# An mLSTM cell feeding a GELU layer: another order of the front's steps, and the second sum of w_out in the middle of the second up projection

## The chip, the cores and the metric

The kernel runs on one core of one Trainium2 chip. The metric is device time in microseconds (us) of one execution. The kernel before has a median of 518.63 us over 11 runs (517.47 to 519.23).

A core has five engines that matter here: TensorE (PE in the profile; its weight loads are shown apart as PEld), VectorE (DVE), ScalarE (ACT), GpSimd (POOL) and SyncE (SP), which here only issues DMAs. Each works through its own queue of instructions in order, and waits on semaphores for the others.

## The reference

Two blocks follow each other. The first is a recurrent cell with batch 4, 8 heads, 768 steps and head size 40:

```python
for t in range(S):
    m_new = np.maximum(f_gate[:, :, t] + m, i_gate[:, :, t])
    f_stab, i_stab = np.exp(f_gate[:, :, t] + m - m_new), np.exp(i_gate[:, :, t] - m_new)
    C = f_stab[:, :, None, None] * C + i_stab[:, :, None, None] * np.einsum('bhd,bhe->bhde', vt, kt)
    n = f_stab[:, :, None] * n + i_stab[:, :, None] * kt
    ...
    y[:, :, t] = sigmoid(o_gate[:, :, t]) * h_tilde / np.maximum(np.abs(nq), 1.0)
```

Its result, as x with 3072 rows of 320, goes through `gelu(x @ w_in) @ w_out` with w_in 320 x 2048 and w_out 2048 x 320. The weights arrive as float64, and the kernel converts them from their bits.

## The kernel before, in words

The 768 steps are cut into six chunks of 128. For each chunk and each of the four batch entries the cell is worked out in matrix form; then the 512 tokens of the chunk (4 x 128) go through the up projection, the GELU and the down projection. The cell of chunk c+1 is worked out beside the down projection of chunk c.

Chunks 1 to 5 use a Strassen-like scheme: `summed_up` makes seven products in place of eight for the up projection, `down_steps` seven for the down projection. These need sums of blocks of w_in (`in_sum`), of x (`sum_x`), of the hidden values (`hidden_sums`) and of w_out (`weight_sum`). Chunk 0 is done with plain products, because the sums aren't there yet.

The first part of the program, called the front below, does all this together: the gates, the conversion of 26 pieces of the weights, the cells of chunks 0 and 1, and both projections of chunk 0. Its order is written out by hand in the string `FRONT`; `play` takes its words one after the other, and each issues instructions on several engines. Every engine's queue therefore has the order of the string. The words are:

- `P n` fetches piece n of the weights; `L n` loads q and k, `O n` loads v and the output gate; `B n` loads a broadcast of the running maxima. All go through SP's queue in this order.
- `E` and `N` work out the gates of the chunks behind the first (each with a store through SP's queue), `D` and `Q` turn the decays (`decays_turned`: transposes on PE, copies on DVE, a product, a copy).
- `K` is the first half of the conversion of the next piece (`conv_one`: three instructions on DVE, two on ACT), `J` the second half (`conv_two`: two on DVE, then the fetch of the piece four further on). Pieces 1 to 10 are w_in (512 columns wide), 11 to 26 are the rows of w_out (320 wide). Below, J4 is the fourth `J`.
- Small letters are the cell of chunk 0 with the batch entry behind them, capitals that of chunk 1: `m` mask (POOL), `w` decay weights (eight exponentials on ACT; in chunk 0 also products on PE), `g` sigmoid of the output gate, `t` transposes of k and q (PE) and their copies (ACT), `s` scores (PE) and their product with the weights (DVE, line 399), `c` state (PE; line 430 on ACT in chunk 0), `v` values (PE), `y` the end of the cell (DVE), `x` the transpose into xT (PE, ACT).
- `A` and `U` are the up projection of chunk 0 for the first and the second half of the tokens, in four steps each (`up_step`, lines 530 to 549). Two steps behind each other are issued together, a single one when the next other word comes. `F` is one of the 16 steps of chunk 0's down projection, `Z` one of the eight sums of w_in.
- `I n` (`keep_clock`) sets how many products of the identity with itself the next word with a PSUM bank makes into that bank ahead of its own work (`unread`, line 315). Nobody reads them. A later `I` ahead of that word overwrites the number. In the string before, 25 products are made that way, two instructions each in the profile.

[...] `ps_mm` has two buffers for each of the tags a and b. The scores of an even batch entry take both buffers of tag a until line 399 has read them, and `U` steps 1 and 3 take the same two; `A` and `U` alternate between a and b. `ps_h` has two buffers for `c` and `v`.

`FRONT` is played once. Then, for each further chunk, come `summed_up` and the string `DOWN`. For chunk 1 the kernel makes `weight_sum(1)` ahead of `summed_up` and `weight_sum(2)` behind it (eight subtractions of 128x160 on DVE each, line 508), and hands out sums 3 and 4 over `DOWN`. `summed_up` works in two groups of two column blocks, (0, 2) and (4, 6); within the second group it makes `hidden_sums` of the first, and at its end those of the second. The second product of the down projection (p6) reads sum 2.

Of the kernel before, what the change touches and what calls it, by code (L numbers as in the profile page):

```python
# [22 lines left out]


FRONT = """
    O0 g0 L0 I6 P0 E I6 I1 P1 I1 w0 t0 I1 I2 I2 L1 I2 N I1 I3 K I1 w1 I5 I2 D Q I6 I3 L2 s0 O2 P2 I3 O1 P3 I5 I1 t1
    I2 I2 w2 c0 I1 J v0 K K s1 I1 L3 I2 I5 w3 I2 t2 I6 I2 I8 I3 I2 I3 I3 y0 O3 v1 J I1 g1 x0 c1 K y1 s2 I7 O4 I1 L4
    I1 B5 t3 g3 I3 J I2 x1 g2 B4 s3 v2 I4 I1 I6 I2 I5 I6 I2 c2 c3 y2 v3 x2 M0 K J y3 G0 L5 O5 A L6 K J J x3 M1 T0 W0
    O6 A K S0 K C0 J H W1 L7 T1 M2 O7 U U M3 K J Z V0 K T2 G1 A J J S1 K C1 Z W2 W3 A J K Z S2 C2 V1 K T3 J K Y0 J U
    U K J Z S3 J G2 Y1 K C3 K Z J F F F K F J J F K Z F J F F G3 K J K X0 K J J B8 K K J J V2 Y2 V3 K J F K X1 F F F  # L30
    F F Y3 Z J Z B9 F X2 X3 F"""
DOWN = """
    M0 Z M1 T0 W0 F F T1 W1 Z G3 Z F S0 Z S1 C0 M2 Z C1 G1 G0 M3 V0 Y0 Z V1 W2 Z F F T2 W3 F T3 F G2 Z Y1 S2 S3 C2
    V2 C3 Y2 V3 F F Y3 X0 F F X1 X2 F F X3 F"""
# [3 lines left out]
def kernel(  # L38
# [18 lines left out]
    B, H, S, D = q.shape  # L57
# [442 lines left out]
    def weight_sum(n):  # L500
        x, y = {1: (Bm[0][1], Bm[0][0]), 2: (Bm[1][1], T[1]), 3: (Bm[1][1], Bm[0][1])}.get(n) or (Bm[1][0], T[2])
        if n == 4:

            parts = [raw.tile([P, 3, HD], F32, name="t4", tag=tag) for tag in ("sig", "pow", "sig")]
            T[4] = lambda j: parts[j // 3][:, j % 3, :]

        def step(j):
            nc.vector.tensor_tensor(out=T[n](j), in0=x(j), in1=y(j), op=OP.subtract)  # L508

        return [lambda j=j: (step(j), step(j + 1)) for j in range(0, HF, 2)]  # L510
# [10 lines left out]
    def hidden_sums(g, f0, f1):  # L521

        (a11, a21), (_, a22) = [[g.t[:, HF * e + f0:HF * e + f1, HT * h:HT * (h + 1)] for h in range(2)]
                                for e in range(2)]
        s1, s2 = [t[f0 // (HF // 2)][:, f0 % (HF // 2):f0 % (HF // 2) + f1 - f0, :] for t in (g.s1, g.s2)]
        nc.vector.tensor_tensor(out=s1, in0=a21, in1=a22, op=OP.add)
        nc.vector.tensor_tensor(out=s2, in0=s1, in1=a11, op=OP.subtract)
        nc.vector.tensor_tensor(out=a21, in0=a11, in1=a21, op=OP.subtract)
# [24 lines left out]
    def first_up_steps(h):  # L553

        def step(k):
            ups.append((len(ups) + len(tags_next) % 2, (2 * k, 2 * k + 2, HT * h, HT * h + HT)))
            if len(ups) == 2:
                first_up()

        return [lambda k=k: step(k) for k in range(HF // 2)]  # L560
# [12 lines left out]
    def in_sum(i):  # L573
        f, (a11, a12), (a21, a22) = slice(WP * (i // 4), WP * (i // 4 + 1)), *[[w_in[:, x, e, :] for x in range(NX)]
                                                                               for e in range(2)]
        s1, s2, s4 = in_sums
        to, x, y, op = ((s1, a21, a22, OP.add), (s2, s1, a11, OP.subtract), (a21, a11, a21, OP.subtract),
                        (s4, a12, s2, OP.subtract))[i % 4]
        nc.vector.tensor_tensor(out=to[:, f], in0=x[:, f], in1=y[:, f], op=op)

    def x_blocks():
        return [[xT[:, x, HT * h:HT * (h + 1)] for h in range(2)] for x in range(NX)]
# [4 lines left out]
        for to, x, y in ((t1, b12, b11), (t2, b22, t1), (b12, b22, b12), (t4, b21, t2)):  # L587
            nc.vector.tensor_tensor(out=to, in0=x, in1=y, op=OP.subtract)

    def summed_up(g):  # L590
        (a11, s3), (a12, a22) = [[w_in[:, x, e, :] for e in range(2)] for x in range(NX)]
        s1, s2, s4 = in_sums
        (b11, t3), (b21, b22) = x_blocks()
        t1, t2, t4 = x_sums
        def product(to, lhs, rhs, f0, first, last):

            for j in range(2):
                nc.tensor.matmul(to[:, j, :], lhs[:, (f0 + j) * P:(f0 + j + 1) * P], rhs, start=(first and j == 0),  # L598
                                 stop=(last and j == 1), skip_group_check=True)

        def products(f0, to_sum):

            blk = [[g.t[:, HF * e + f0:HF * e + f0 + 2, HT * h:HT * (h + 1)] for h in range(2)] for e in range(2)]
            c11, c12, c21, c22 = [pool.tile([P, 2, HT], F32, name="pu", tag=tag)
                                  for pool, tag in ((ps_tr, "tr"), (ps_h, "h"), (ps_mm, "a"), (ps_mm, "b"))]
            product(c11, a11, b11, f0, True, False)
            nc.scalar.copy(out=blk[1][1], in_=c11)  # L607
            product(c12, s2, t2, f0, True, True)
            nc.vector.tensor_tensor(out=blk[0][0], in0=c12, in1=blk[1][1], op=OP.add)  # L609
            product(c21, s1, t1, f0, True, True)  # L610
            nc.vector.tensor_tensor(out=blk[0][1], in0=c21, in1=blk[0][0], op=OP.add)
            product(c22, s3, t3, f0, True, False)
            nc.vector.tensor_tensor(out=blk[1][0], in0=c22, in1=blk[0][0], op=OP.add)
            if to_sum > 0:
                hidden_sums(g, f0 - 4, f0 - 2)
            product(c11, a12, b21, f0, False, False)
            product(c12, s4, b22, f0, True, False)
            product(c21, a22, t4, f0, True, False)
            return f0, blk, ((c11, c21), (c12, c22))

        def rest(f0, pair, h):
            for j in range(2):
                for e in range(2):
                    nc.tensor.matmul(pair[e][:, j, :], w_rest[halves[e], (f0 + j) * P:(f0 + j + 1) * P],  # L624
                                     xT[halves[e], NX, HT * h:HT * (h + 1)], start=False, stop=(j == 1),
                                     skip_group_check=True)

        for group in ((0, 2), (4, 6)):

            sets = [products(f, group[0]) for f in group]  # L630
            for h in range(2):
                for f, _, pairs in sets:
                    rest(f, pairs[h], h)
            for _, blk, ((c11, _), _) in sets:
                nc.scalar.activation(out=blk[0][0], in_=c11, func=AF.Gelu)  # L635
            add_to = lambda blk, e, h, x, y: (
                nc.vector.tensor_tensor(out=blk[e][h], in0=x, in1=y, op=OP.add),  # L637
                nc.scalar.activation(out=blk[e][h], in_=blk[e][h], func=AF.Gelu))  # L638
            for _, blk, ((_, c21), _) in sets:
                add_to(blk, 1, 0, c21, blk[1][0])  # L640
            for _, blk, (_, (c12, c22)) in sets:
                add_to(blk, 1, 1, c22, blk[0][1])
                add_to(blk, 0, 1, c12, blk[0][1])
        hidden_sums(g, HF - 4, HF)
# [4 lines left out]
    def first_down_steps(g):  # L649
        po = []  # L650

        def row(f):

            if f == 0:
                po.extend(ps_mm.tile([P, DM], F32, name="po", tag="ab"[b // 2]) for b in range(B))
            for b in range(B):
                nc.tensor.matmul(po[b], g.t[:, f, b * L:(b + 1) * L], w_out[:, f, :], start=(f == 0),  # L657
                                 stop=(f == NF - 1))
                if f == NF - 1:
                    if b % 2 == 0:  # L660
                        o_sb = outp.tile([P, 2, DM], F32, name="o_sb", tag="o_sb")
                    nc.scalar.copy(out=o_sb[:, b % 2, :], in_=po[b])
                    send(0, b, o_sb[:, b % 2, :])

        return [lambda f=f: row(f) for f in range(NF)]
# [71 lines left out]
    def in_turn(steps):  # L737
        todo = list(steps)
        return lambda: todo.pop(0)() if todo else None

    def cell_steps(c, letters):
# [8 lines left out]
                 A=in_turn(first_up_steps(0)), U=in_turn(first_up_steps(1)), F=in_turn(first_down_steps(first_g)),  # L750
                 K=in_turn(lambda i=i: conv_one(i) for i in n_pieces), H=sums_begin,
                 J=in_turn(lambda i=i: conv_two(i) for i in n_pieces), Z=in_turn(lambda i=i: in_sum(i) for i in range(8)))
    steps |= cell_steps(0, "mwgtscvyx") | cell_steps(1, "MWGTSCVYX")
    play(FRONT, steps)
    for c in range(1, NCH):
        g, later = Hidden(True), []
        if c == 1:
            for step in weight_sum(1):
                step()
        summed_up(g)  # L760
        if c == 1:
            for step in weight_sum(2):
                step()
            later = weight_sum(3) + weight_sum(4)
        steps = dict(F=in_turn(down_steps(c, g)), Z=in_turn(later))
        if c + 1 < NCH:
            steps |= cell_steps(c + 1, "MWGTSCVYX")
        play(DOWN if c + 1 < NCH else "F " * 14, steps)
# [30 lines left out]
```

## Time and profile before

| what | value |
|---|---|
| median of 11 runs | 518.63 us |
| the profiled execution | 517.57 us, of which the profile's span is 515.8 us |
| PE busy | 501.2 us (97%) |
| DVE busy | 342.5 us (66%) |
| ACT busy | 253.0 us (49%) |
| front (to the first product of `summed_up`) | 0 to 133.19 us |
| chunks 1 to 5 | 133.19 us to the end |
| granted TensorE clock, mean | 0.993 |

All times below are from the start of the span. A row of the list of instructions in order of time has the start, the duration, the engine, the line, the operation, the output and the inputs, the shapes, the number of instructions, and in brackets how long the engine sat idle before and what released it. Matmuls overlap, so that a row's duration is longer than the distance to the next row; sums are made with the distances. The chain of work that ended last gives start, duration, engine and line.

### The profile page before, as it was taken

How to read it: one execution, taken by the hardware profiler on the slowest of the kernel's cores; microseconds unless marked ns; L12 is line 12 of the kernel's file. 1: busy time of each engine (PE TensorE's matmuls, PEld its weight loads, DVE VectorE, ACT ScalarE, POOL GpSimd, SP SyncE). 2: the span in 40 equal slices, each digit the busy share in tenths (PEclk: the TensorE clock that was granted, in tenths of full speed). 3: DMA queues.
4: the chain of work that ended last, by engine and by line, in shares of the span. 5: the costliest groups of instructions: out<-in, count | busy, mean ns of one | idle time of the engine just before them, and what ended most of it. 6: DMA issues, size and time to landing. Idle time of an engine off the chain costs nothing.

```text
span 515.8 us, 10990 instructions
## 1 busy us (share of the span) xinstructions
PE 501.2 (97%) x4486; PEld 452.0 (88%) x4486; DVE 342.5 (66%) x696; ACT 253.0 (49%) x522; POOL 61.2 (12%) x98
## 2 busy tenths in 40 slices
PE   4899999999999999999999999999999999999997
PEld 3787888777888999988999988999988999988997
DVE  7689888999667987347668347678337657237621
ACT  7695999543344960152980132982123882124300
POOL 3001000001200235000045000053000021000000
PEclk9799999999999999999999999999999999999999
DMA  8999971259800244900124910124920020000001
GB/s 174 182 172 200 209 170 50 81 155 223 139 0 1 84 112 60 169 0 2 63 97 67 167 31 1 42 83 81 164 54 2 3 80 2 27 27 0 1 2 51
DMA packets 111442, 41.62 MB, mean 81 GB/s; under 512 B 101184, under 2 KB 104416, under 8 KB 111392
## 3 DMA queue, kind: packets, MB, share of 16 engines
q1 hardware_dynamic: 111392, 40.92, 37.8%
q8 instruction: 35, 0.57, 0.5%
q14 instruction: 15, 0.12, 0.1%
HBM read 36.90 MB, written 4.01 MB: 79 GB/s over the span
## 4 chain that ended last, share of the span: by engine, by line
PE 90%; DVE 6%; ACT 2%; issue 1%; DMA 0%; SPq 0%; DVEq 0%
PE po L680 29%; PE pu L598 24%; PE pu L624 7%; PE po L657 7%; PE pu L539 5%; PE ps L396 4%; PE ph L445 4%; PE pt L374 3%; PE pf L420 2%; PE pf L415 2%; PE pu L545 1%; PE px L471 1%; DVE M L195 1%; DVE g L637 1%; DMA i_sb<-in_i_gate_dram 0%
## 5 line engine op out<-in xcount | busy, mean ns | idle before, releaser
L680 PE MATMUL po<-w_out,g 128*128 128x160 f32 x640 | 91.5, 299 | 0.0
L680 PEld LDWEIGHTS po<-w_out,g 128*128 128x128 f32 x640 | 88.0, 190 | 0.3 <-DVE g L637 0.3
L598 PE MATMUL pu<-xT,w_in 128*128 128x256 f32 x240 | 58.9, 381 | 0.0
L637 DVE TENSOR_TENSOR g<-pu,g 128x512 f32<-128x512 f32 x60 | 40.5, 690 | 24.3 <-PE pu L624 22.8
L598 PEld LDWEIGHTS pu<-xT,w_in 128*128 128x128 f32 x240 | 45.0, 190 | 7.5 <-ACT g L638 1.7
L360 ACT ACTIVATE W<-Mb,aT 128x128 f32<-128x128 f32 x160 | 48.9, 391 | 0.1
L472 ACT COPY xT<-px 128x384 f32<-128x384 f32 x24 | 10.9, 476 | 76.9 <-PE px L471 76.9
L680 PE MATMUL po<-w_sums,sums 128*128 128x160 f32 x320 | 47.4, 302 | 0.3 <-DVE w_sums L508 0.3
L399 DVE TENSOR_TENSOR W<-ps,W 128x512 f32<-128x512 f32 x48 | 30.3, 685 | 22.1 <-PE ps L396 20.4
L680 PEld LDWEIGHTS po<-w_sums,sums 128*128 128x128 f32 x320 | 44.0, 190 | 0.9 <-DVE w_sums L508 0.5
L335 POOL TENSOR_SCALAR_AFFINE_SELECT Mb<-Mb 128x1024 f32<-128x1024 f32 x20 | 22.6, 1138 | 174.3 <-DMA Mb<-M_d 169.2
L607 ACT COPY g<-pu 128x512 f32<-128x512 f32 x20 | 11.6, 581 | 58.2 <-PE pu L598 58.2
L693 DVE TENSOR_TENSOR o_sb<-po,o_sb 128x320 f32<-128x320 f32 (+1 forms) x27 | 12.5, 463 | 39.8 <-PE po L680 36.2
L598 PE MATMUL pu<-x_sums,in_sums 128*128 128x256 f32 x160 | 37.8, 379 | 0.0
L635 ACT ACTIVATE g<-pu 128x512 f32<-128x512 f32 x20 | 11.9, 597 | 52.7 <-PE pu L624 52.7
L624 PE MATMUL pu<-xT,w_rest 64*128 64x256 f32 x320 | 37.2, 382 | 0.0
L638 ACT ACTIVATE g<-g 128x512 f32<-128x512 f32 x60 | 36.1, 627 | 1.9
L609 DVE TENSOR_TENSOR g<-pu,g 128x512 f32<-128x512 f32 x20 | 13.8, 691 | 34.4 <-PE pu L598 28.6
L624 PEld LDWEIGHTS pu<-xT,w_rest 64*128 64x128 f32 x320 | 30.1, 187 | 6.4 <-issue 3.3
L657 PE MATMUL po<-w_out,g 128*128 128x320 f32 x128 | 35.3, 434 | 0.0
L598 PEld LDWEIGHTS pu<-x_sums,in_sums 128*128 128x128 f32 x160 | 30.2, 190 | 4.3
L657 PEld LDWEIGHTS po<-w_out,g 128*128 128x128 f32 x128 | 24.0, 190 | 9.6
(144 smaller groups left out, 889.4 us busy)
## 6 DMA issues: line engine op xcount, KB each, us to landing
Mb<-M_d SPq DMA_DIRECT2D x20, 512.0 KB, 3.9
bits<-in_moe_w_in_dram SPq DMA_DIRECT2D x20, 256.0 KB, 4.3
bits<-in_moe_w_out_dram SPq DMA_DIRECT2D x16, 320.0 KB, 3.1
vb<-in_v_dram SPq DMA_DIRECT2D x24, 160.0 KB, 5.1
ob<-in_o_gate_dram SPq DMA_DIRECT2D x24, 160.0 KB, 3.8
qb<-in_q_dram SPq DMA_DIRECT2D x24, 160.0 KB, 4.4
kb<-in_k_dram SPq DMA_DIRECT2D x24, 160.0 KB, 4.8
out_dram<-o_sb SPq DMA_DIRECT2D x24, 160.0 KB, 2.8
```

Source lines behind the costliest of these rows:

```text
L335: nc.gpsimd.affine_select(out=t, in_=t, compare_op=OP.is_ge, fill=1.0e30, base=0, pattern=[[0, H], [1, L]], channel_multiplier=-1)
L360: nc.scalar.activation(out=W[n][:, h, :], in_=src, func=AF.Exp, scale=-1.0, bias=aT[:, self.c, r:r + 1])
L396: nc.tensor.matmul(ps[hip][:, p, :], kT[r, p, :], qT[r, p, :], start=True, stop=True)
L399: nc.vector.tensor_tensor(out=w, in0=ps[hip], in1=w, op=OP.mult)
L445: nc.tensor.matmul(ph[r, h, :], Pm[:, h, r], vb[n % NLD][:, h, :], start=True, stop=True)
L539: nc.tensor.matmul(banks[-1][e][:, i - i0, :], w_in[:, x, e, i * P:(i + 1) * P], xT[:, x, t0:t1], start=(x == 0 and i == i0), stop=False, ...
L598: nc.tensor.matmul(to[:, j, :], lhs[:, (f0 + j) * P:(f0 + j + 1) * P], rhs, start=(first and j == 0), stop=(last and j == 1), skip_group_c ...
L624: nc.tensor.matmul(pair[e][:, j, :], w_rest[halves[e], (f0 + j) * P:(f0 + j + 1) * P], xT[halves[e], NX, HT * h:HT * (h + 1)], start=False ...
L637: nc.vector.tensor_tensor(out=blk[e][h], in0=x, in1=y, op=OP.add),
L638: nc.scalar.activation(out=blk[e][h], in_=blk[e][h], func=AF.Gelu))
L657: nc.tensor.matmul(po[b], g.t[:, f, b * L:(b + 1) * L], w_out[:, f, :], start=(f == 0), stop=(f == NF - 1))
L680: nc.tensor.matmul(bank[at][:, i, :], lhs(j, t), rhs(j), start=(first and i == 0 and j == 0), stop=(i == n - 1 and j == HF - 1), skip_grou ...
```

## The change

The string `FRONT` is another one. It has the same 181 steps besides the `I` words, in another order, and 10 `I` words in place of 45, with a total of 18 unread products that are really made in place of 25. They stand ahead of other steps: one at `w0` as before, none from there to `v1`, then three at `v1`, five at `c1`, two at `s2` and seven at `c2`.

`weight_sum(2)` is called from inside `summed_up` for chunk 1, in the first group, behind the third VectorE sum of its second column block, in place of behind the whole of `summed_up`.

```diff
 FRONT = """
-    O0 g0 L0 I6 P0 E I6 I1 P1 I1 w0 t0 I1 I2 I2 L1 I2 N I1 I3 K I1 w1 I5 I2 D Q I6 I3 L2 s0 O2 P2 I3 O1 P3 I5 I1 t1
-    I2 I2 w2 c0 I1 J v0 K K s1 I1 L3 I2 I5 w3 I2 t2 I6 I2 I8 I3 I2 I3 I3 y0 O3 v1 J I1 g1 x0 c1 K y1 s2 I7 O4 I1 L4
-    I1 B5 t3 g3 I3 J I2 x1 g2 B4 s3 v2 I4 I1 I6 I2 I5 I6 I2 c2 c3 y2 v3 x2 M0 K J y3 G0 L5 O5 A L6 K J J x3 M1 T0 W0
-    O6 A K S0 K C0 J H W1 L7 T1 M2 O7 U U M3 K J Z V0 K T2 G1 A J J S1 K C1 Z W2 W3 A J K Z S2 C2 V1 K T3 J K Y0 J U
-    U K J Z S3 J G2 Y1 K C3 K Z J F F F K F J J F K Z F J F F G3 K J K X0 K J J B8 K K J J V2 Y2 V3 K J F K X1 F F F
-    F F Y3 Z J Z B9 F X2 X3 F"""
+    O0 L0 I1 I1 g0 E L1 P0 O2 P1 w0 t0 N D K w1 L2 P2 Q P3 s0 O1 t1 w2 L3 c0 J K v0 K s1 y0 w3 t2 I3 g1 v1 O3 I2 I3
+    I5 J c1 B5 I2 K y1 I4 I2 s2 x0 O4 L4 t3 J x1 B4 s3 v2 I7 g3 L5 g2 c2 c3 y2 v3 x2 O5 L6 K J G0 A y3 x3 J H M0 M1
+    K K J T0 W0 O6 M2 O7 A J W1 S0 C0 K J T1 L7 U U K Z K V0 T2 A M3 J J G1 S1 K W2 W3 K C1 Z A S2 Z V1 G2 J Y0 J K
+    C2 Z T3 J K Y1 U U J S3 Z V2 C3 K J K K J J F K F F F Z J K J X0 K K J F F F Z J F K G3 Y2 F J K V3 J K F K X1 J
+    J F F F F K Z X2 B8 J F Y3 X3 B9 F"""
...
-    def summed_up(g):
+    def summed_up(g, sums_too):
...
             if to_sum > 0:
                 hidden_sums(g, f0 - 4, f0 - 2)
+            elif f0 > 0:
+                for step in sums_too:
+                    step()
             product(c11, a12, b21, f0, False, False)
...
-        summed_up(g)
+        summed_up(g, weight_sum(2) if c == 1 else [])
         if c == 1:
-            for step in weight_sum(2):
-                step()
             later = weight_sum(3) + weight_sum(4)
```

## The prediction

> **What bounds the kernel now.** I read the page's first parts, then the busy time by stretch, then the chain of work that ended last, and last the instructions in order of time where the change has its steps.
>
> The page's busy shares, and its row of the granted clock in 40 slices (tenths behind the name PEclk):
>
> ```profile
> PE 501.2 (97%) x4486; PEld 452.0 (88%) x4486; DVE 342.5 (66%) x696; ACT 253.0 (49%) x522; POOL 61.2 (12%) x98
> PEclk9799999999999999999999999999999999999999
> ```
>
> PE is full except at the start. The busy time by stretch (start:end, length, PE, PEld, DVE, ACT, POOL, clock, DMA) shows how long that start is:
>
> ```profile
> 10.00:15.00 5.00, 3.12 (x26) 2.33 (x24) 4.73 (x13) 3.62 (x9) 0.00 (x0) 0.91 0.86 159
> 15.00:20.00 5.00, 4.12 (x21) 3.67 (x23) 1.47 (x7) 2.87 (x10) 0.00 (x0) 0.50 1.23 193
> 20.00:25.00 5.00, 5.00 (x62) 4.31 (x58) 3.53 (x7) 2.52 (x8) 0.00 (x0) 0.91 1.02 195
> 30.00:35.00 5.00, 5.00 (x83) 4.49 (x82) 4.17 (x11) 4.93 (x13) 0.00 (x0) 1.00 0.60 137
> 35.00:40.00 5.00, 4.39 (x68) 3.98 (x68) 4.50 (x10) 3.48 (x7) 0.00 (x0) 1.00 1.14 208
> 40.00:45.00 5.00, 4.17 (x77) 3.69 (x76) 4.79 (x13) 2.21 (x6) 0.00 (x0) 1.00 0.62 234
> ```
>
> The clock is at half from 14 to 21 us; until 45 us DVE and ACT set the pace (ACT 4.93 of 5.00 between 30 and 35), and PE has holes, part of them filled with unread products. The chain then stays on PE:
>
> ```profile
> 50.41 3.29 PE pu L539 x14
> ...
> 57.87 6.91 PE pu L539 x32
> ...
> 95.03 17.42 PE po L657 x64
> ...
> 133.19 12.09 PE pu L598 x56
> ...
> 164.06 0.70 DVE g L637
> ...
> 171.40 2.44 PE po L680 x16
> ...
> 245.00 1.02 PE pt L374 x8
> ```
>
> So from the start of A1 (43.76 us) to 133.19 the front is PE work: 89.43 us, with one hole of about 0.43 (A2 takes 5.14 from 49.63 to 54.77 where A1-like steps take 4.71, waiting for J5). The steps are the same in the new order, so PE's work behind A1 stays at 89.0 us. Two questions remain: when A1 starts, and which new holes come behind it.
>
> **Part 1, the sums of w_out.** The rows of DVE that matter:
>
> ```profile
> 146.42 0.69 DVE L637 TENSOR_TENSOR g<-pu,g 128x512 f32<-128x512 f32 x1 [3.00 <-PE pu L624]
> 171.03 1.97 DVE L508 TENSOR_TENSOR w_sums<-w_out,w_sums 128x160 f32<-128x160 f32 x8
> ```
>
> Eight instructions, 1.97 us, stand between the last `hidden_sums` and the product p6. The new place is a hole of 3.00 us on DVE, ahead of 146.42; 1.03 us of it stay empty, and only line 637 is queued behind. Without that cover they would cost up to 1.97 us. What they save: by the chain, chunk 1 goes from 164.80 (first transpose behind `summed_up`, after 0.74 on line 637) to 245.00, 80.20 us; the next two stretches like it, 245.00 to 324.58 and 324.58 to 404.16, are 79.58. So the gain is at most 0.62 us, and at least 0. I take 0.6: the later chunks differ by just these sums (and sums 3 and 4, which DVE then starts two us earlier).
>
> **Part 2, from the gates to A1.**
>
> ```profile
> 18.08 1.49 PE L317 MATMUL ps<-ident 128*128 128x128 f32 x6
> 19.49 1.84 PE L396 MATMUL ps<-qT,kT 64*128 64x128 f32 x16
> 22.22 0.58 ACT L377 COPY kT<-pt 128x512 f32<-128x512 f32 x1 [4.33 <-PE pt L374]
> 33.65 1.16 PE L396 MATMUL ps<-qT,kT 64*128 64x128 f32 x16
> 37.48 1.16 PE L396 MATMUL ps<-qT,kT 64*128 64x128 f32 x16 [0.61 <-ACT qT L377]
> 40.43 0.67 PE L415 MATMUL pf<-vw,kb 128*64 128x41 f32 x16
> ```
>
> - s0 loses its three unread products: 18.08 to 19.49, 1.41 us of PE at half clock. Against that, D now stands ahead of K1 and w1 behind D. DVE then does the copies of D at 13.74, waits 0.73 for its product as before, and K1 (1.40) ends near 16.4; PE does w1 at half clock, about 1.9 us as w0 (7.49 to 9.6), and Q comes some 0.5 later. s0 starts about 0.9 earlier.
> - t1 loses one product (0.2). The copy of kT1, at 22.22 before, comes near 21.15. From there ACT runs without a hole until 38.5 in the old order, and the new one gives it the same instructions up to t3 (w2, c0, K2, K3, w3, t2, g1 with a table load, c1, K4, x0, t3). So s3 comes about 1.0 earlier, at 36.45 for 37.48. DVE is no bound: it comes to y1, which waited 0.69 for g1, about 1.0 earlier too.
> - c2 now has seven products, 14 instructions at 0.11 us (ten took 1.11, from 27.05 to 28.16) = 1.54. s3 and v2 end near 38.55, so c2 starts near 40.1 (40.43 before, where it had two and waited 0.27 for vw). Of the 1.0 us, 0.3 is left: A1 starts near 43.45. Ends: if the seven were free, 1.0; if ACT gets stuck on w1, whose exponentials come 1 us later, 0.3 is lost.
> - Queues: on SP, P0 now stands behind E's store (7.36) and L1 (1.0 us); with 4.3 us to landing it is there near 13.9, and K1 needs it near 15.0. O6, O7 and the fetch of J7 stand behind the load that waits for W0, 1.3 us later than before; K11 needs that piece near 76. On POOL the masks M0 and M1 move behind J5; the first took place at 45.2 and W0 needs it at 55. Cost 0; without the 1.1 us of slack K1 would push Q and s0 by what is missing.
>
> **Part 3, behind A1.**
>
> ```profile
> 53.57 2.45 ACT L360 ACTIVATE W<-Mb,aT 128x128 f32<-128x128 f32 x8
> 55.76 1.29 DVE L399 TENSOR_TENSOR W<-ps,W 128x512 f32<-128x512 f32 x2 [1.58 <-ACT W L360]
> 57.70 2.54 PE L539 MATMUL pu<-xT,w_in 128*128 128x256 f32 x11
> ```
>
> - J5 comes ahead of K6, M0 and T0; DVE has it near 47, A2 starts near 49.4. The hole of 0.43 goes.
> - K7 now stands ahead of W0 on ACT (it was behind A2). A1's GELU ends 5.8 us behind A1's start (43.76, 49.56), at 49.25. Then x3 0.46, K6 and K7 at 1.45, T0 1.07, a table load 1.28, seven of W0's eight exponentials 2.15: 57.1. Line 399 on the scores of s0 of chunk 1 takes 0.6 for its first half, and only then has U1 a buffer of tag a, at about 57.9. PE comes there at 43.45 + 4.71 (A1) + 0.35 (x3) + 0.9 (T0) + 4.71 (A2) + 0.9 + 1.19 (C0) + 1.02 (T1) = 57.2. A new hole of 0.7 us at U1. Behind line 399 wait C0's sums, K8 and J8; J8 is needed only at the end of A3 (near 73), and I find it near 66. Ends: 0 and 1.5 (a K more).
> - V2 stands ahead of F1 instead of behind F8, G2 ahead of the last `U` pair (one more table load on ACT, 1.28). Its GELU ends near 96.5; F1 needs the third bank near 97. DVE is 3 us ahead of each F by its sums (J15 near 102, F5 near 105; J26 near 127, F16 near 131). Cost 0; uncovered, the table load would cost up to 1.28.
>
> **The sum.** -0.3 (A1) -0.43 (J5) +0.7 (U1) -0.6 (sums) = -0.65 us against the profiled execution: 517.57 - 0.65 = 516.9. That execution is 1.06 us under the median, so in medians 518.63 - 0.65 = 518.0. A measurement of this kernel can tell about 0.2% (1.04 us) from no change, so this is within it. The own range of this case is -1.7 to +0.5: 516.9 to 519.1.
>
> [...] The row first: scores of 16 instructions take 1.84 at half clock and 1.16 at full, and the stretch from 14 to 21 us is at half although PE was recorded busy for 3.12 of 5 us ahead of it. [...] By the row the new order, with PE about as busy from 17.5 to 21 us as now, ends the half clock at the same time, and the sum is as above. [...]
>
> **The rivals.**
>
> 1. The clock drops again (slower). Between 20 and 45 us 20 unread products were made, now 17, but none until 27, and between 33 and 36.5 only x0, t3, x1 and a wait of about 1.4 us for ACT, with nothing to fill it. For: 3.12 busy of 5.00 was not enough at 10 to 15. Against: 4.17 and 4.39 of 5.00 were enough between 35 and 45. Price: a half-clock stretch as in the rows is 6.8 us long (0.09 of 5, all of 5 at half, 0.09 of 5); it costs half of that, 3.4, less the holes that it swallows (0.61 + 0.83): 2.0 to 3.4. It decides from 1.7 us of loss on. With 2.7: -0.65 + 2.7, 520.7.
> [...]
> 3. ACT becomes the bound between 50 and 58: another 1.5 us in the hole at U1, and line 399 late by as much; +0.85, 519.5.
> 4. The moved sum does nothing, since another wait (0.44 at line 420 in every chunk) takes its place: -0.05, 518.6.
>
> **How the numbers follow.** Main case 0.39 (of it 0.11 under -1.04 and 0.01 over +1.04), rival 1 0.29, rival 2 0.20, rival 3 0.08 (0.03 over +1.04), rival 4 0.04. Faster: 0.11 + 0.20 = 0.31. Slower: 0.29 + 0.03 + 0.01 = 0.33. Same: 0.27 + 0.05 + 0.04 = 0.36. The range goes from 515.9 (rival 2 with free products at c2, -0.7 more, and a spread of 0.2) to 521.4 (rival 1 with its upper price).
>
> **What would show it.** s0 near 18.6 and the copy of kT1 near 21.1; c2 behind 14 unread instructions; A1 at 43.2 to 43.8; at U1 PE waiting for line 399 with W0's exponentials ending at 57; no wait for line 508 on PE near 171; the stretch from the transposes behind `summed_up` of chunk 1 to those of chunk 2 at 79.6. Wrong would make it: a clock under 1.00 between 22 and 45, K1 waiting for its piece, or F steps waiting for J.

## The result, and the profile after

| | before | after |
|---|---|---|
| median | 518.79 us (49 runs, 517.15 to 519.61) | 517.32 us (13 runs, 516.51 to 518.07) |
| ratio of the times, 95% | | 0.9974, 0.9966 to 0.9982 |
| the profiled execution | 517.57 us | 516.78 us |
| its span | 515.8 us | 515.0 us |

The ratio is worked out from the single executions of both kernels and isn't quite the quotient of the two medians (517.32 / 518.79 would be 0.9972); the same holds for the ratios below. By it, the changed kernel is faster by 0.26%, about 1.35 us (1.47 in medians), which is a little more than the 0.2% that a measurement of this kernel can tell from no change. The pair of profiled executions shows less, 0.79 us; the reason is in the start of the kernel, and is shown below.

The page of after, busy shares and granted clock:

```profile
PE 499.8 (97%) x4472; PEld 450.2 (87%) x4472; DVE 339.9 (66%) x696; ACT 254.6 (49%) x523; POOL 60.3 (12%) x98
PEclk9799999999999999999999999999999999999999
```

PE is still what is full. 4472 matmuls for 4486 are the seven unread products less, two instructions each. The busy time by stretch of after (start:end, length, PE, PEld, DVE, ACT, POOL, clock, DMA share, GB/s):

```profile
10.00:15.00 5.00, 3.03 (x21) 2.46 (x20) 4.14 (x15) 3.29 (x9) 0.00 (x0) 0.95 1.09 228
15.00:20.00 5.00, 4.62 (x32) 3.47 (x31) 2.26 (x7) 3.50 (x10) 0.00 (x0) 0.50 1.10 241
20.00:25.00 5.00, 5.00 (x84) 4.33 (x84) 4.22 (x8) 3.42 (x12) 0.00 (x0) 0.87 1.14 223
...
35.00:40.00 5.00, 3.79 (x63) 3.38 (x62) 4.56 (x9) 2.53 (x6) 0.00 (x0) 1.00 0.95 180
40.00:45.00 5.00, 4.72 (x81) 4.22 (x80) 4.73 (x15) 2.68 (x7) 0.78 (x1) 1.00 1.08 250
```

The clock is at half once, from about 14.5 to 21.3 us, and at 1.00 from there on, although PE now has more holes between 35 and 40 (3.79 busy for 4.39). Between 15 and 20 PE is fuller: 4.62 for 4.12.

The chain of work that ended last (start, duration, engine, output, line, count):

```profile
57.37 7.17 PE pu L538 x32
...
95.75 8.81 PE po L659 x32
...
132.98 12.09 PE pu L597 x56
...
164.66 1.02 PE pt L373 x8
...
170.91 2.18 PE po L682 x16
...
244.24 1.02 PE pt L373 x8
```

DVE's line of the sums, a link of this chain at 171 us before, is gone from it: PE goes from the transposes behind `summed_up` of chunk 1 to those of chunk 2 in 244.24 - 164.66 = 79.58 us, in place of 80.20. The rows of before that the next ones are compared with, besides those in the prediction:

```profile
43.76 3.62 PE L539 MATMUL pu<-xT,w_in 128*128 128x256 f32 x16
...
133.03 1.03 PE L598 MATMUL pu<-xT,w_in 128*128 128x256 f32 x4
```

So the first product of `summed_up` starts at 133.03; the 133.19 named ahead of the prediction and in it is a link of the chain a little behind that start, and 89.43 us from A1 is rightly 89.27. The instructions of after in order of time, first those up to A1, then those around U1, then the sums:

```profile
18.52 2.08 PE L395 MATMUL ps<-qT,kT 64*128 64x128 f32 x16
21.57 0.58 ACT L376 COPY kT<-pt 128x512 f32<-128x512 f32 x1 [2.61 <-PE pt L373]
36.48 1.16 PE L395 MATMUL ps<-qT,kT 64*128 64x128 f32 x16 [1.22 <-ACT qT L376]
38.63 1.83 PE L316 MATMUL pf<-ident 128*128 128x128 f32 x14
40.39 1.13 PE L414 MATMUL pf<-vw,kb 128*64 128x41 f32 x32
43.25 3.62 PE L538 MATMUL pu<-xT,w_in 128*128 128x256 f32 x16
...
49.12 3.62 PE L538 MATMUL pu<-xT,w_in 128*128 128x256 f32 x16
54.43 2.45 ACT L359 ACTIVATE W<-Mb,aT 128x128 f32<-128x128 f32 x8
56.62 1.29 DVE L398 TENSOR_TENSOR W<-ps,W 128x512 f32<-128x512 f32 x2 [2.63 <-ACT W L359]
57.37 7.17 PE L538 MATMUL pu<-xT,w_in 128*128 128x256 f32 x32 [0.46 <-DVE W L398]
...
143.12 1.97 DVE L507 TENSOR_TENSOR w_sums<-w_out,w_sums 128x160 f32<-128x160 f32 x8
146.21 0.69 DVE L639 TENSOR_TENSOR g<-pu,g 128x512 f32<-128x512 f32 x1 [1.12 <-PE pu L626]
```

The balance of the pair: A1 0.51 us earlier (43.76 to 43.25); A2 in one piece (49.12), with no wait for J5; at U1 PE waits 0.46 for line 398, which waited for the exponentials of W0. From A1 to the first product of `summed_up` it is 89.57 us, where it was 89.27, so that the first product comes 0.21 earlier (133.03 to 132.82); then 0.62 on the sums, which fill the hole ahead of line 639 (3.00 before, 1.12 now). Together 0.83.

### The half clock comes in whole pieces of 3.4 us

To compare single executions of the front, three things are read from each (the runs named here are described in the next section): the origin (the four transposes of `a` on PE, lines 183 to 185, which start at 11.36 to 12.00 us), where the half clock lies, and the first product of `summed_up`. Busy time by stretch, before:

```profile
14.00:15.00 1.00, 0.00 (x0) 0.00 (x0) 0.96 (x3) 1.00 (x2) 0.00 (x0) 0.56 0.86 143
...
20.00:21.00 1.00, 1.00 (x14) 1.00 (x12) 0.00 (x0) 0.00 (x0) 0.00 (x0) 0.53 1.21 166
```

A clock of 0.56 in the stretch from 14 means that the half clock starts at 14.12; 0.53 in that from 20 means that it ends at 20.94: 6.82 us. The same reading of the changed front with the old place of the sum (the run e2_front_only):

```profile
15.00:16.00 1.00, 1.00 (x10) 0.59 (x8) 0.96 (x3) 0.86 (x2) 0.00 (x0) 0.56 0.93 308
...
21.00:22.00 1.00, 1.00 (x8) 0.81 (x7) 1.00 (x2) 0.73 (x2) 0.00 (x0) 0.53 1.01 248
```

15.12 to 21.94, again 6.82. In after it is 14.46 to 21.28; in the run e6_s0_three below 14.04 to 24.28, which is 10.24; in e5_no_unread there is another one from 32.76 to 36.16, 3.40. These are one, two and three times 3.41; the expectations below call one such piece a window. In a third kind of execution the start never comes to full clock: PE's short matmuls keep their half-clock duration (0.63 where the full one is 0.38) until 22.5 to 24.0, while the clock column shows 1.00. e9_before_j5, whose front is that of before up to A1, is one of these:

```profile
13.07 0.63 PE L357 MATMUL pm<-beyond,eye 128*128 128x512 bf16 x1
...
24.14 0.38 PE L357 MATMUL pm<-beyond,eye 128*128 128x512 bf16 x1
```

So executions of one kernel differ by where the half clock lies, and fronts are compared at places that are alike, if not the same (from the origin it starts at 2.62 in before and 2.75 in after, at 3.19 in e1 and 3.61 in e2):

| half clock | old front: A1, first product, from the origin | new front | difference |
|---|---|---|---|
| from 14.1 / 14.5 (before / after) | 32.26, 121.53 | 31.54, 121.11 | -0.72, -0.42 |
| from 15.2 / 15.1 (e1 / e2) | 32.50, 121.88 | 31.47, 121.03 | -1.03, -0.85 |
| all of the start (e9 / e4, e11) | 33.27 | 32.52, 32.52 | -0.75 |

The new front reaches A1 0.7 to 1.0 us earlier. The profiled after started its origin 0.21 later than the profiled before (11.71 and 11.50), which hides as much of the gain in the plain difference.

The times say the same. The mean granted clock of an execution tells the number of half-clock pieces that it recorded (two of them are 3.41 us lost of some 516: 0.993; one: 0.997; three: 0.990; none recorded: 0.999 or 1.0). Medians of the executions with like mean clock, with their number:

| mean clock | before, beside all experiments | before, beside e1 and e2 | sum alone (e1) | front alone (e2) | both |
|---|---|---|---|---|---|
| 0.997 | 517.23 (13) | 517.22 (6) | 516.67 (3) | none | none |
| 0.993 | 518.44 (49) | 518.16 (13) | 517.80 (7) | 517.58 (4) | 516.55 (5) |
| 0.990 to 0.992 | none | none | none | 518.13 (1) | 516.99 (3) |
| 0.999 or 1.0 | 519.03 (45) | 519.01 (16) | 518.80 (2) | 518.12 (7) | 517.71 (6) |

Against the before that was measured beside them, the sum is worth 0.55, 0.36 and 0.21 in its three rows, and the front 0.58 and 0.89 in its two. Both together were measured at another time, beside a before whose clocks aren't on record. The groups are small, so these are sizes and no proof.

The first and third row hold something else. The number of pieces goes with the order of the front: of the 167 executions with the old front (before, e1, e8, e9, e10, e12) 26 have a mean clock of 0.996 or 0.997, one piece, and none is under 0.993; of the 76 with the new front and most of its unread products (after, e2, e3, e4, e6, e7, e11) none has one piece, and 18 are at 0.989 or 0.990, three pieces. In the changed kernel the one execution with three pieces takes 517.85 us, where the middle of those with two is 516.55, so the new front pays back a part of its gain in some executions. Why it does wasn't looked into.

### The profile page after: what moved, and what is told of

Its sections match the earlier page's. It is cut to its first block, busy times and chain, and to the rows that moved or that the text cites. A ratio compares the mean times of both kernels' runs of the same rounds, so it can differ in the third digit from the quotient of the medians.

```text
span 515.0 us, 10957 instructions
## 1 busy us (share of the span) xinstructions
PE 499.8 (97%) x4472; PEld 450.2 (87%) x4472; DVE 339.9 (66%) x696; ACT 254.6 (49%) x523; POOL 60.3 (12%) x98
## 4 chain that ended last, share of the span: by engine, by line
PE 91%; DVE 3%; DMA 2%; ACT 2%; SPq 1%; issue 1%; DVEq 0%; ACTq 0%
PE po L682 30%; PE pu L597 24%; PE pu L626 7%; PE po L659 7%; PE pu L538 5%; PE ph L444 4%; PE ps L395 4%; PE pt L373 3%; PE pf L419 2%; PE pf L414 2%; PE px L470 1%; PE pu L544 1%; DMA bits<-in_moe_w_in_dram 1%; DMA vb<-in_v_dram 1%; SPq L271 1%
```

## The experiments

### Which of the two parts

e1_sum_only: the old `FRONT`, and only the sum moved.

```diff
-    def summed_up(g):
+    def summed_up(g, sums_too):
...
+            elif f0 > 0:
+                for step in sums_too:
+                    step()
...
-        summed_up(g)
+        summed_up(g, weight_sum(2) if c == 1 else [])
```

> The order of the front of before, with the second sum of w_out inside the second up projection. Theory (the two parts add up, each as its own rows say): the stretch from the transposes behind the second up projection to those of the third goes from 80.20 to 79.58 us, the front stays at 133.19, so -0.6 us against before. Rival (the sum is most of the change, and the front is only re-arranged): -1.2 us or more in the medians, nearly all of the measured -1.35.

Measured: 517.70 us, before 518.58 beside it; ratio 0.9983 (0.9972 to 0.9995). Its chain:

```profile
165.72 1.02 PE pt L374 x8
...
245.30 1.02 PE pt L374 x8
```

Again 79.58 us: the sum's mechanism and its size, 0.62, stand without the new front.

e2_front_only: the new `FRONT`, and the sum behind `summed_up`.

```diff
 FRONT = """
-    O0 g0 L0 I6 P0 E I6 I1 P1 I1 w0 t0 I1 I2 I2 L1 I2 N I1 I3 K I1 w1 I5 I2 D Q I6 I3 L2 s0 O2 P2 I3 O1 P3 I5 I1 t1
...
+    O0 L0 I1 I1 g0 E L1 P0 O2 P1 w0 t0 N D K w1 L2 P2 Q P3 s0 O1 t1 w2 L3 c0 J K v0 K s1 y0 w3 t2 I3 g1 v1 O3 I2 I3
...
```

> The changed order of the front, with the sum behind the up projection as before. Theory: the first product of the second up projection comes near 132.98 (133.19 before), so -0.2 us in a profiled execution, and PE again waits for line 508 near 171. Rival (the front's order gains more than the one profiled pair shows, because it meets the half clock at the start better in most executions): -0.8 us in the medians.

Measured: 518.08 us, before 518.58; ratio 0.9997 (0.9986 to 1.0007). PE waits 0.3 us for the sums of line 507 again, ahead of this link of the chain:

```profile
170.91 2.44 PE po L679 x16
```

By the ratio of this run alone the front could be worth nothing; the trace (0.85 to the first product, against e1 with its half clock 0.4 us earlier from the origin) and the executions of like mean clock (0.58 and 0.89) say otherwise. The medians of the two parts, 0.88 and 0.50, add up to the 1.35 of the whole within their uncertainty.

### Where the front gains

e6_s0_three: the changed kernel with three unread products ahead of s0 again.

```diff
-    ... w1 L2 P2 Q P3 s0 O1 t1 ...
+    ... w1 L2 P2 Q P3 I3 s0 O1 t1 ...
```

> The changed kernel with the three unread products ahead of s0 that the kernel before has there. Theory (they stand on PE at half clock ahead of s0 and push all that follows, 1.41 us in the profile before): s0, the copy of kT1 and A1 come about 1.0 to 1.4 us later, the time is 1.0 us longer than the changed kernel's. Rival (they bring the clock up one window earlier and pay for themselves): A1 within 0.3 of the changed kernel's, the time the same.

Measured: 518.72 us, before 518.63; ratio 0.9995 (0.9984 to 1.0007). In order of time:

```profile
18.78 1.49 PE L316 MATMUL ps<-ident 128*128 128x128 f32 x6
20.20 2.08 PE L395 MATMUL ps<-qT,kT 64*128 64x128 f32 x16
```

The three cost 1.42 us of PE at half clock, and the median goes up by 1.40 against the changed kernel, by 0.75 (516.55 to 517.30) among executions at a mean clock of 0.993. So these three products, put back into the stretch at half clock, take away about as much as the whole front gains. Not all of it need be their own time: the half clock of this profile has three pieces (14.04 to 24.28), and 4 of the 12 executions have a mean clock of 0.989 or 0.990, where the changed kernel has 1 of 14 (but e3 and e4 below, without these products, have 4 and 5 of 12).

e8_before_s0_free was meant as the counterpart, before without them. Two of its products stayed, because the `I5 I2` ahead of `D` still asked for them; so it takes out one of three.

```diff
-    ... K I1 w1 I5 I2 D Q I6 I3 L2 s0 O2 ...
+    ... K I1 w1 I5 I2 D Q L2 s0 O2 ...
```

> The kernel before without the three unread products ahead of s0, and with nothing else changed. Theory (these six instructions are most of what the front gained): A1 about 1.0 us earlier for the same end of the half clock, the time 0.7 to 1.0 us shorter than before. Rival (ScalarE, with kT1 behind w1, sets the pace, or the clock rises a window later without them): the time within 0.4 us of before.

Measured: 518.58 us, before 518.63; ratio 0.9998 (0.9988 to 1.0008). From the origin s0 comes 0.44 earlier than in e1, which has the old front, but s1 (14.70, 14.72) and A1 (32.49, 32.50) come at the same time. A part of this is the clock's: from the origin the half clock lies at 3.66 to 10.48 in e8 and at 3.19 to 10.03 in e1, with PE empty until 4.00 in both, so that it takes about 0.2 us more of e8 (an estimate, half of 0.45). And a new loss appears, in order of time:

```profile
43.78 2.75 POOL L335 TENSOR_SCALAR_AFFINE_SELECT Mb<-Mb 128x1024 f32<-128x1024 f32 x2 [38.43 <-DMA Mb<-M_d]
...
44.00 1.58 DVE L298 SCALAR_TENSOR_TENSOR pow<-bits,pow 128x512 uint32<-128x512 uint32 x1
45.61 1.46 DVE L303 SCALAR_TENSOR_TENSOR w_in<-sig,pow 128x512 f32<-128x512 f32 x1
...
51.52 3.29 PE L539 MATMUL pu<-xT,w_in 128*128 128x256 f32 x14 [1.06 <-DVE w_in L303]
```

Two steps of J on DVE take 1.58 and 1.46 us beside the masks on POOL, where they take 0.68 and 0.69 otherwise. From the origin J5 ends 0.75 later than in e1 (39.96, 39.21), and A2 waits 1.06 for it in place of 0.30.

e9_before_j5: before, with J5 ahead of the second K.

```diff
-    ... A L6 K J J x3 M1 T0 W0
+    ... A L6 J K J x3 M1 T0 W0
```

> The kernel before with J5 ahead of K6 in place of behind it, and nothing else. Theory (VectorE's order sets the start of A2, so that the hole there, 0.43 us with the half clock ending at 20.9 and more when A1 comes earlier, goes): A2 runs without a wait for line 303, the front ends 0.4 us earlier, 0.4 us shorter than before. Rival (line 399 on the scores of chunk 1 takes the hole over at U1): the front ends where it did.

Measured: 518.55 us, before 518.71; ratio 0.9997 (0.9987 to 1.0008). The wait at A2 is gone (16 instructions in one row), but the 0.43 us that it was worth can't be seen in the times, and hardly in the trace: from A1 to the first product it is 89.19 us, 0.08 less than in before. S1 takes back most of it, 1.35 for 1.06:

```profile
73.78 1.35 PE L396 MATMUL ps<-qT,kT 64*128 64x128 f32 x16
```

e10_before_j5_s0: both, this time with all three products out.

```diff
-    ... K I1 w1 I5 I2 D Q I6 I3 L2 s0 O2 ...
+    ... K I1 w1 D Q L2 s0 O2 ...
...
-    ... A L6 K J J x3 M1 T0 W0
+    ... A L6 J K J x3 M1 T0 W0
```

> The kernel before with J5 ahead of K6 and with no unread product at all ahead of s0. Theory (both are needed: without the products A1 comes earlier, and only with J5 early is that kept): s0 at or before 18.6, A1 0.9 to 1.2 us earlier for the same end of the half clock, no wait at A2, the front 1.2 to 1.6 us shorter, as with the changed order: -1.2 us against before in the medians. Rival (the clock needs the products): the half clock ends a window (3.4 us) later, and the time is that of before or longer.

Measured: 517.56 us, before 518.71; ratio 0.9984 (0.9973 to 0.9994). Against e1, from the origin, s0 comes 1.29 earlier (6.72, 8.01), A1 0.44, and the first product 0.63 (121.25, 121.88), with the half clock as late as in e8 (3.65 to 10.47). That is less than expected at A1 and in the front, since here too it is 89.19 from A1 on. Still, two edits in the old order give a gain of the size that the whole new front gives (0.85 to the first product in the trace of e2, 0.50 in its median); which of the other moves matter is left open.

e12_mended_sum: e10 and the moved sum.

```diff
-    ... K I1 w1 I5 I2 D Q I6 I3 L2 s0 O2 ...
+    ... K I1 w1 D Q L2 s0 O2 ...
...
-    ... A L6 K J J x3 M1 T0 W0
+    ... A L6 J K J x3 M1 T0 W0
...
+            elif f0 > 0:
+                for step in sums_too:
+                    step()
...
-        summed_up(g)
+        summed_up(g, weight_sum(2) if c == 1 else [])
```

> The kernel before with J5 ahead of K6, with no unread product ahead of s0, and with the second sum of w_out inside the second up projection. Theory (the parts add up): -1.15 us of the front and -0.6 of the sum, about 1.7 us shorter than before, a little shorter than the changed kernel. Rival (they overlap): -1.2 us.

Measured: 517.81 us, before 518.98; ratio 0.9973 (0.9961 to 0.9984). That is 1.17 in medians, less than the sum of e10 (1.15) and e1 (0.88). By the ratio it is as fast as the changed kernel (0.9974): three small edits do what the new string does. In its profile lines 298 and 303 take 1.58 and 1.46 us again, from 44.62, as beside the masks in e8, PE waits 0.57 for ACT inside A2, and the half clock fills all of the start; how often the masks meet J there isn't known.

### The unread products and the clock

e3_c2_free: the changed kernel without the unread products ahead of c2.

```diff
-    ... B4 s3 v2 I7 g3 L5 g2 c2 c3 ...
+    ... B4 s3 v2 g3 L5 g2 c2 c3 ...
```

> The changed kernel without the seven unread products at c2. Theory (they cost time because c2 could start at 39.4 in place of 40.39): A1 starts near 42.5 in place of 43.25, the hole at U1 stays, -0.75 us against the changed kernel. Rival 1 (they hold the clock up): the granted clock falls below 1.00 between 35 and 45 us, and the time is 1 to 3 us longer than the changed kernel's. Rival 2 (c3 and v3 wait for ScalarE's copies anyway): A1 within 0.2 of 43.25, no difference.

Measured: 517.46 us, before 518.58; ratio 0.9984 (0.9973 to 0.9995), in the median no better than with them; among the executions at 0.999 or 1.0 it is 517.42 (8) for 517.71 (6). In order of time:

```profile
40.10 0.67 PE L414 MATMUL pf<-vw,kb 128*64 128x41 f32 x16 [0.72 <-DVE vw L382]
41.51 0.67 PE L414 MATMUL pf<-vw,kb 128*64 128x41 f32 x16 [0.75 <-ACT state L429]
...
57.95 7.17 PE L538 MATMUL pu<-xT,w_in 128*128 128x256 f32 x32 [0.82 <-DVE W L398]
```

Without the products PE waits 0.72 for vw at c2 and 0.75 for ACT's copies at c3. From s3 to A1 it takes 6.28 us (37.15 to 43.43), where it takes 6.77 in after (36.48 to 43.25): of the 1.76 us of the seven products (38.63 to 40.39) 0.49 is a cost, and the rest is time in which PE would have waited. The half clock fills the start in this profile as in e4 and e11, which have the products; A1 comes 0.6 earlier than there (31.92 from the origin, 32.52), of which 0.25 is there already at s1 (13.57, 13.82), ahead of the products. The hole at U1 takes 0.4 back (89.97 from A1 to the first product, 89.57 in after). The clock stays at 1.00.

e5_no_unread: the changed kernel without any.

```diff
-    O0 L0 I1 I1 g0 E ... t2 I3 g1 v1 O3 I2 I3 I5 J c1 B5 I2 K y1 I4 I2 s2 ... v2 I7 g3 ...
+    O0 L0 g0 E ... t2 g1 v1 O3 J c1 B5 K y1 s2 ... v2 g3 ...
```

> The changed kernel without any unread product. Theory (behind the first rise of the clock PE is busy enough by itself): the clock stays at 1.00 from about 23 us on, A1 comes at most 0.3 us earlier than in the changed kernel, because c3 and v3 wait for ScalarE's copies, and the time is within 0.5 us of it. Rival (the products hold the clock up): a stretch under 1.00 between 25 and 45 us, A1 2 to 3.4 us later, the time longer by as much.

Measured: 518.26 us (516.93 to 520.92), before 518.63; ratio 1.0002 (0.9988 to 1.0015). The busy time by stretch:

```profile
30.00:35.00 5.00, 3.56 (x40) 3.32 (x41) 3.89 (x11) 4.90 (x12) 0.00 (x0) 0.78 0.80 241
35.00:40.00 5.00, 3.71 (x56) 3.23 (x54) 4.53 (x10) 3.13 (x7) 0.00 (x0) 0.88 0.97 180
```

Here the clock falls back, for one piece of 3.4 us, behind PE's wait of 2.35 us for vw, and two of the twelve executions are above 520. In the changed kernel 6 of 14 executions have a mean clock of 0.999 or 1.0, here none of the twelve, and the median is 0.94 higher. So the remaining unread products do hold the clock in the changed kernel; the danger that the prediction saw in the new order is real, a few products further on. The profile itself, of the fastest of the twelve, shows the fall but little loss by it: A1 comes 32.02 behind the origin, as in e7 below, which has no fall, with s1 0.2 us ahead of e7's.

### The hole at U1, and an order without it

e4_k7_back: the changed kernel with K7 behind A2 and J7 later.

```diff
-    K K J T0 W0 O6 M2 O7 A J W1 S0 C0 K J T1 L7 U U ...
+    K J T0 W0 O6 M2 O7 A K W1 S0 C0 J K J T1 L7 U U ...
```

> The changed kernel with K7 behind A2 again, and J7 behind C0. Theory (K7 on ScalarE ahead of W0's exponentials makes the hole at U1): W0's exponentials end near 55.4 in place of 56.9, line 398 follows at once, U1 starts when PE comes to it near 56.9, V0 near 65.8 in place of 66.4; -0.7 us against the changed kernel. Rival (the hole only moves to a later step, because J7 and J8 are then late for A3): V0 at 65.8, but PE waits for line 302 at A3 near 68, and the time is the same or longer.

Measured: 517.23 us, before 518.58; ratio 0.9977 (0.9966 to 0.9987). In order of time:

```profile
56.02 1.29 DVE L398 TENSOR_TENSOR W<-ps,W 128x512 f32<-128x512 f32 x2 [1.20 <-ACT W L359]
57.52 7.07 PE L538 MATMUL pu<-xT,w_in 128*128 128x256 f32 x32
...
72.95 1.44 PE L395 MATMUL ps<-qT,kT 64*128 64x128 f32 x16
```

PE no longer waits at U1. Half of that is lost at S1, which takes 1.44 where it took 1.06, because the copies of T2 on ACT come at 72.13 for 71.36. From A1 to the first product it is 89.22 us, 0.35 less than in after.

e7_both: e4 and e3 together.

```diff
-    ... B4 s3 v2 I7 g3 L5 g2 c2 c3 ...
+    ... B4 s3 v2 g3 L5 g2 c2 c3 ...
...
-    K K J T0 W0 O6 M2 O7 A J W1 S0 C0 K J T1 L7 U U ...
+    K J T0 W0 O6 M2 O7 A K W1 S0 C0 J K J T1 L7 U U ...
```

> The changed kernel with K7 behind A2, J7 behind C0, and without the seven products at c2. Theory (each alone is held up by the other: with c2 free the hole at U1 grows, with K7 back A1 sets the pace): A1 0.25 us earlier than in the changed kernel for the same clock, no hole at U1, 0.4 us lost at S1 as with K7 alone, so -0.5 us against the changed kernel. Rival (the gains don't add): -0.3 us, as with K7 alone.

Measured: 517.23 us, before 518.63; ratio 0.9972 (0.9961 to 0.9982). In the medians the products at c2 make no difference. In the traces they do: e7 and e4 differ in nothing else and both have the half clock over all of the start, and from the origin A1 comes 32.02 and 32.52, the first product 121.26 and 121.74. Up to s1 they are alike (13.84 and 13.82), so that the 0.5 us is the products'.

e11_k7_k10: the edit of e4, and the K ahead of V0 moved behind T2.

```diff
-    ... T1 L7 U U K Z K V0 T2 A M3 ...
+    ... T1 L7 U U K Z V0 T2 K A M3 ...
```

> The changed kernel with K7 behind A2, J7 behind C0, and K10 behind T2. Theory (with K7 back ScalarE's copies of T2 came 0.4 us too late for S1; with K10 behind them they don't): S1 takes 0.9 us in place of 1.3, U1 without a hole, -0.7 us against the changed kernel. Rival (J10 is then late for A4, or another step is): -0.35 us, as with K7 alone.

Measured: 516.87 us (515.82 to 517.35), before 518.71; ratio 0.9965 (0.9951 to 0.998). In order of time:

```profile
70.99 0.56 ACT L376 COPY kT<-pt 128x512 f32<-128x512 f32 x1
...
73.18 1.06 PE L395 MATMUL ps<-qT,kT 64*128 64x128 f32 x16
```

T2's copies come in time, S1 takes 1.06 again, and from A1 to the first product it is 88.84 us: 0.73 less than in the changed kernel, by the trace. The times place it below before for certain; against the changed kernel (0.9974) the intervals overlap, though among the executions at 0.999 or 1.0 it is 516.97 (6) for 517.71 (6).

## Why the prediction was right and where it was wrong

The predicted time was 518.0 and the measured one 517.32, inside the range. The likeliest case gave a gain too small to be told from none, 0.65 us; it was twice that. The direction was right, the size was not.

- **The sums of w_out** (-0.6): right. The stretch went from 80.20 to 79.58 here and in e1, and DVE's hole took the eight instructions whole. Rival 4, that another wait takes their place, fell.
- **J5** (-0.43): right. A2 has no wait, and in e11, where U1 and S1 have no hole either, all of it is there (88.84 from A1 on for 89.27). In the old order the same move alone gained 0.08 (e9), because S1 came to wait.
- **U1** (+0.7): right in mechanism and size, though its own terms, 57.1 and 0.6, make 57.7 and not 57.9. The exponentials of W0 ended at 56.88 (57.1 predicted), PE waited for line 398, and from S0 to V0 it took 12.76 in place of 12.04. From A1 to the first product the two terms make 89.27 - 0.43 + 0.7 = 89.54; measured 89.57.
- **A1** (-0.3): this term of the sum was mis-sized. It measured -0.51 in the pair, and -0.72, -1.03 and -0.75 from the origin at three places of the half clock. The steps up to s3 held within about 0.4 us (s0 18.52 for 18.6, the copy of kT1 21.57 for 21.15, s3 36.48 for 36.45). What failed is "c2 starts near 40.1 [...] Of the 1.0 us, 0.3 is left", which prices the seven products at 0.7. They cost 0.5: from s3 to A1 it takes 6.77 or 6.78 us in the five profiles with them and 6.26 to 6.28 in the nine without them (before and the runs with its front, which have two there, and e3, e5 and e7). Their own time was taken too short (1.54 for 1.76, since ten of before take 1.22 to the next matmul and not 1.11), so that c2 started at 40.39; but A1 came 2.86 behind it and not 3.33 as before. The products were priced as work put on top. Before, PE waited twice there, and the second time is this row in order of time:

```profile
41.84 0.67 PE L415 MATMUL pf<-vw,kb 128*64 128x41 f32 x16 [0.75 <-ACT state L430]
```

  The seven products ran while ACT came to this point, c3 followed c2 without a break (one row of 32), and of 0.75 only 0.28 was left, one step later. The prediction knew of the hole of c3 (it took it off the price of rival 1) but left it in the way from c2 to A1. Of the 1.0 us at s3 not 0.3 but 0.5 was left in the pair, and 0.72 of 1.21 from the origin.
- **The profiled execution of before** was taken as a plain sample, 1.06 us under the median. It was one in which the half clock lies well for the old order: it starts at 14.12, and PE is empty until 15.50, waiting for gT. So 1.38 us of it fall into a wait, and in e1 0.81 (15.18 to 15.99). The half clock then ends 0.59 later from the origin in e1 (10.03, 9.44), s0 takes 2.08 for 1.84 (the 1.84 that the prediction reads as half clock is partly at full), and A1 comes 0.24 later (32.50, 32.26). With its origin 0.49 later and its front 0.35 longer, e1 shows 0.84 of the 1.06 us. In the new order w1 fills that time, and gains if the half clock starts later. In order of time, before, then e2 (half clock from 15.12), then after (from 14.46):

```profile
15.50 0.63 PE L215 MATMUL pd<-gT,last 128*128 128x32 f32 x2 [1.97 <-DVE gT L186]
```

```profile
14.35 0.39 PE L354 MATMUL pm<-M_parts,row 96*128 96x128 bf16 x4
```

```profile
14.64 0.61 PE L354 MATMUL pm<-M_parts,row 96*128 96x128 bf16 x4
```

  w1's groups take 0.39 at full clock and 0.61 to 0.63 at half, and s0 lies 6.02 behind the origin in e2, 6.81 in after, 7.99 and 8.01 in before and e1. This is why the median gained more than the pair: to the first product the front gains 0.42 (before and after) or 0.85 (e1 and e2) from the origin, and with the 0.62 of the sums that makes -1.04 to -1.47.
- **The rivals.** The clock did not drop again in the profile of the changed kernel (rival 1), but in e5, without the unread products, it did, for one piece of 3.4 us where the prediction had priced 6.8. For rival 2's 0.20 and the lower end of the range, 515.9, the clock would have had to rise earlier, which no run of the new front shows: in the profile of after it was half for two pieces, as before (6.82 us), and none of the 76 executions counted above has the single piece that 26 of 167 of the old front have. ACT as the bound around U1 (rival 3) added nothing beyond the term of U1.

What isn't settled: why the new front has three pieces of half clock in some executions and the old one never; which moves besides the three products ahead of s0 and J5 matter; how often the masks meet J; and whether e11's 0.73 us against the changed kernel are there in the times, since the two weren't measured beside each other.

## What to carry to other kernels

Work that fills a wait costs only what goes over the wait (0.5 of 1.76 us here): before adding a filler's duration to the path, follow the path to the next wait on the same engine and take off what the filler swallows there. Where the clock of the first microseconds differs between executions (half from 14.12 in before, from 15.18 in e1 with the same front), compare executions from a common origin and with the slow stretch at the same place; one pair of profiles showed 0.79 of 1.35 us here. Filler work in a stretch at half clock cost nearly double here (1.42 us for six instructions, 0.76 at full clock in before, 30.48 to 31.24), so take it out there first, and keep it where its removal lets the clock fall (e5, 0.50 from 32.76 to 36.16).

## What the runs showed of the hardware that wasn't expected

- The half clock lasted whole numbers of pieces of 3.41 us (3.40, 6.82, 10.24), at places that differ between executions (from 14.04 in e6, 14.12 in before, 15.18 in e1); in some profiles (e9 for one) the clock column showed 1.00 over the start while matmuls of 0.38 us took 0.63.
- Where two selects on POOL (line 335, 1.09 us each at the median in before) ran side by side with DVE's operations of lines 298 and 303, both were longer, in e8: 2.75 us for the two selects, and 1.58 and 1.46 for 0.68 and 0.69 (e12 has the same 1.58 and 1.46). In e1, where line 303 had started 0.44 us ahead of the selects (45.22, 45.66), it kept its 0.69.
- With the clock at 1.00 and no unread product behind it, one wait of 2.35 us on PE was followed by a fall to half (e5, with PE at work for 1.33 of the 3.41 us ahead of the fall); waits of 1.22 to 1.3 were not (after, e2, and e3, where PE is busy for only 2.74 of the 5 us from 35 on).
